# A second searched sequence for the tasks of a fused attention and state-space kernel on one core

## Chip, core, metric

The kernel runs on one core of a Trainium2 chip. The core has engines that work at the same time, each through its own list of instructions in a fixed order: TensorE (PE, matrix products; PEld is its weight load), VectorE (DVE), ScalarE (ACT), GpSimd (POOL) and SyncE (SP). The last two mostly issue transfers here. The metric is the time of one execution on the device in microseconds (us), lower is better. Three runs of the kernel before took 327.48, 326.56 and 324.36 us; the median is 326.56.

## What is computed

Two branches read the same `x` of 2,048 positions and 640 channels, and a gate mixes them. Branch A is attention over eight keys at distances 0, 2, ..., 14; branch B is a long convolution whose filter comes from 192 complex states per channel.

```python
g = sigmoid((x * gate_w).sum(-1, keepdims=True))

# A: 32 heads of 20; query s sees the keys s - 2*w, w = 0..7
q, k, v = split_heads(x @ wqkv)
idx = arange(2048)[:, None] - 2 * arange(8)[None, :]
logits = where(idx >= 0, einsum("hsd,hswd->hsw", q, k[idx]) * 20 ** -0.5, -1e9)
a = merge_heads(einsum("hsw,hswd->hsd", softmax(logits), v[idx])) @ wo

# B: K[d, l] = Re sum_n C[d,n] dB[d,n] exp(dt A[d,n] l), then y = x * K + x Dskip
dt = exp(log_dt)[:, None]
K = einsum("dn,dnl,dn->dl", C, exp((dt * A)[:, :, None] * arange(2048)), dt * B).real
b = irfft(rfft(pad(x)) * rfft(pad(K)))[:, :2048] + x * Dskip

out = g * a + (1 - g) * b
```

## The kernel before

The program is cut into tasks. Each builder adds tasks to a plan by `Plan.add`: a name, the engine or engines that may make it, the function that writes its instructions, the tasks it must follow, and the buffers it takes and frees. There are two plans, "main" with 1,258 tasks and "tail" with 304. Nothing at build time decides the sequence: `ORDER` (L54) holds, for each plan, one string of differences between task numbers. `Plan.order` walks it, and a letter behind a number names the engine (A is ACT, D is DVE, S is SP, G is POOL) where it isn't the task's first one:

```python
for x in ORDER[self.name].split():
    at += int(x.rstrip("ADSG"))
    t = self.tasks[at]
    t.eng = x[-1] if x[-1] in "ADSG" else next(iter(t.dur))
```

`Plan.emit` (L152) writes the instructions in that sequence and chains those of each engine, so the string fixes every engine's list. Ahead of an ACT task whose function is not in the table set that is loaded (exponential and logarithm in one, sine and arctangent in the other), it writes a table load (L160).

What the tasks of the main plan do, in the rough order of the data:

- *Projections.* x and the weights come into `bufA` by SP, x in four chunks of 512 positions. PE multiplies them into the PSUM tile `tb` (L284, five matmuls of 128x512 a tile), and ACT or DVE copies the tile to `qr`, `kr` or `prj` (q, k, v; `evict`, L476 on ACT and L478 on DVE). A small copy `kr<-kr` carries the last 14 keys of one block of 256 positions to the next.
- *Attention* of a block: `prod` = q times shifted k on DVE (L343), summed over a head by PE into `lg` (L349), row maximum (`mx`, `hi`, `lo`, L365 to L369), exponential into `at` on ACT (L377), row sums and 1/sum on PE and DVE (L381, L385), a way through DRAM by SP that spreads the weights over partitions (`asb`, L391 and L396), `pv` = weights times v on DVE (L417; v is loaded as `vc` by POOL, L337), summed by PE (L424), multiplied by `wo` (L448), and scaled by the gate into `ga` (L457 on ACT, L459 on DVE), which SP stores (L469).
- *State-space parameters.* DVE and ACT work out the size and angle of each state's factor from A, B, C and dt in tiles of 128x960 (builders L591 to L599, called from L639 to L691). The results, split into digits, are the pieces `pc` (L630 and others), which SP stores to `Sprm` in DRAM (L623). Ten chunks of 64 channels load them back as `L` (L734).
- *Filter.* Per chunk PE makes arguments from `L` into PSUM (`ar`, two buffers, L769), ACT takes sines of them into `big` or `bufA` (L784) and exponentials into `big` (L786), DVE multiplies these to `pt` and `qq` (L806, L808), and PE sums over the states in runs of 16 or 32 small matmuls of 32x21 into `kps` (L824), which is evicted to `E`. When five chunks are done, their half of the filter goes by way of DRAM (`Kx`) into `kc` (L907).
- *First transform step* of the filter and of x on PE into `bp` (L1276, L1295), evicted to `big` and `bufA`.

The tail plan holds the rest of the transforms: forward (`fp`, L1043, evicted to `sp_k` and `sp_u`), product of spectra on DVE (L1071, L1074), inverse (L1104, L1134), and the mix with the gate, `ga` and `Dskip` (L1140 to L1148), from which `ot` goes to the output (L1161).

PSUM tiles are few: two `ar`, two `tb` (shared by projections, gathers and output products), one `lg`, one for `kps`. So who frees a tile, and when, sets which engine waits.

## Time and profile before

| | us |
|---|---|
| three runs | 327.48, 326.56, 324.36 |
| median | 326.56 |
| span of the profiled execution | 323.2 |
| projections on PE (L284, 275 matmuls of that shape) | 73.4 |
| sines on ACT into `big` (L784, 72) | 56.1 |
| exponentials on ACT (L786, 60) | 50.4 |
| `prod` on DVE (L343, 40) | 47.8 |
| `pv` on DVE (L417, 40) | 47.6 |
| arguments on PE (L769, 600) | 47.1 |
| `pt` and `qq` on DVE (L806 48, L808 24) | 32.1 + 21.2 |
| `kps` matmuls on PE (L824, 2,560) | 28.1 |
| table loads on ACT (L160, 14) | 18.0 |

The span reaches from the first to the last thing that the profiler recorded on the core. A row of a view names engine, line, operation, output and inputs, and how often it stands there; then busy time and mean duration, or start and length, and in brackets the idle time ahead of it with what ended it ("issue" where nothing that the profile shows did). Line numbers are those of the kernel before; in the changed kernel all lines behind the table are two higher.

### The profile page before, as it was taken

The numbers are of one execution on the slowest core, as the hardware profiler recorded it, in microseconds if no ns is written. First come the engines' busy times: TensorE is split into PE (matmuls) and PEld (weight loads), VectorE is DVE, ScalarE is ACT, GpSimd is POOL, SyncE is SP. The second block draws the span as 40 slices with busy tenths as digits, with TensorE's granted clock in tenths as the row PEclk, the third lists the DMA queues.
The fourth block names the chain that finished last, engine by engine and source line by source line (L and its number), as shares of the span: only waits on it lengthen the run. The fifth ranks groups of instructions, "written<-read, shape, count | busy, mean of one in ns | idle before, by whom it ended". The sixth has DMA issues, their size and how long they took to land.

```text
span 323.2 us, 11733 instructions
## 1 busy us (share of the span) xinstructions
PE 278.4 (86%) x5109; PEld 170.3 (53%) x5134; DVE 294.0 (91%) x408; ACT 281.5 (87%) x425; POOL 62.8 (19%) x94
## 2 busy tenths in 40 slices
PE   0599997999979999999998979889999999997750
PEld 0145543444545645546554545457678776657740
DVE  4888999899998999999999989898998999999891
ACT  1479678999989999999999999899988599996991
POOL 8500026501100000111134523320200000000063
PEclk9999999999999999999999997999999999997995
DMA  8997356662414102467774996533860593962057
GB/s 213 338 227 224 122 173 138 130 128 83 92 30 109 37 6 74 81 161 254 179 190 97 161 179 141 108 96 77 254 258 33 151 312 95 204 123 44 2 135 194
DMA packets 48697, 45.65 MB, mean 141 GB/s; under 512 B 28590, under 2 KB 42482, under 8 KB 48646
## 3 DMA queue, kind: packets, MB, share of 16 engines
q1 hardware_dynamic: 42524, 27.82, 33.7%
q0 software_dynamic: 5216, 16.39, 20.8%
q8 instruction: 40, 0.66, 0.9%
q10 hardware_dynamic: 906, 0.69, 0.7%
q14 instruction: 11, 0.09, 0.1%
HBM read 28.25 MB, written 14.01 MB: 131 GB/s over the span
## 4 chain that ended last, share of the span: by engine, by line
PE 48%; ACT 39%; issue 5%; DVE 3%; SPq 2%; DMA 2%; POOL 0%; POOLq 0%; ACTq 0%; DVEq 0%
PE tb L284 14%; ACT big L784 8%; PE fp L1043 7%; PE ar L769 7%; ACT big L786 6%; PE kps L824 5%; ACT bufA L476 4%; PE tb L424 4%; PE tb L448 4%; ACT L160 3%; PE bp L1276 3%; ACT tt L1140 2%; ACT bufA L784 2%; ACT sp_k L476 2%; DMA bufA<-in_A_wqkv_dram 2%
## 5 line engine op out<-in xcount | busy, mean ns | idle before, releaser
L284 PE MATMUL tb<-bufA 128*128 128x512 bf16 x275 | 73.4, 394 | 6.5 <-DMA bufA<-in_A_wqkv_dram 2.9
L784 ACT ACTIVATE big<-ar 128x740 bf16<-128x740 int16 (+1 forms) x72 | 56.1, 849 | 2.4 <-PE ar L769 1.9
L786 ACT ACTIVATE big<-ar 128x848 bf16<-128x848 f32 x60 | 50.4, 919 | 3.2 <-PE ar L769 3.0
L769 PE MATMUL ar<-Rarg,L 64*128 64x212 bf16 (+4 forms) x600 | 47.1, 253 | 6.3 <-ACT big L784 2.5
L284 PEld LDWEIGHTS <-bufA 128*128 128x128 bf16 x300 | 32.3, 121 | 35.2 <-issue 12.0
L417 DVE TENSOR_TENSOR pv<-vc,asb 128x2048 bf16<-128x2048 bf16 x40 | 47.6, 1217 | 1.1 <-DMA vc<-vS 0.9
L343 DVE TENSOR_TENSOR prod<-qr,kr 128x2048 bf16<-128x2048 bf16 x40 | 47.8, 1218 | 0.5 <-PE lg L349 0.5
L769 PEld LDWEIGHTS <-L 64*128 64x128 bf16 x600 | 22.3, 95 | 35.0 <-issue 32.1
L806 DVE TENSOR_TENSOR pt<-big 128x1024 bf16<-128x1024 bf16 x48 | 32.1, 701 | 1.5 <-PE kps L824 0.8
L824 PE MATMUL kps<-qq,pt 128*32 128x21 bf16 (+1 forms) x2560 | 28.1, 175 | 3.3 <-issue 3.1
L824 PEld LDWEIGHTS <-pt 128*32 128x32 bf16 (+1 forms) x2560 | 23.4, 91 | 12.2 <-issue 10.1
L448 PE MATMUL tb<-wo_sb,oTm 128*128 128x320 bf16 x160 | 27.1, 300 | 0.1
L337 POOL DMA_DIRECT2D vc<-vS x16 | 11.5, 727 | 70.6 <-DVE pv L417 65.4
L476 ACT ACTIVATE sp_u<-fp 128x640 bf16<-128x640 f32 x29 | 22.4, 883 | 2.1 <-PE fp L1043 2.1
L476 ACT ACTIVATE sp_k<-fp 128x640 bf16<-128x640 f32 x30 | 22.7, 878 | 1.0 <-PE fp L1043 0.8
L424 PE MATMUL tb<-pv,ind 128*64 128x512 bf16 (+1 forms) x192 | 22.7, 359 | 0.3 <-ACT qr L476 0.2
L808 DVE TENSOR_TENSOR qq<-big 128x1344 bf16<-128x1344 bf16 x24 | 21.2, 884 | 0.0
L1043 PEld LDWEIGHTS <-PHI 128*128 128x128 bf16 x160 | 15.6, 97 | 8.1 <-issue 1.5
L1161 POOL DMA_DIRECT2D out_dram<-ot x14 | 7.8, 562 | 54.9 <-DVE ot L1143 54.9
L448 PEld LDWEIGHTS <-oTm 128*128 128x128 bf16 x160 | 14.5, 98 | 7.3 <-issue 2.7
L160 ACT ACT_TABLE_LOAD x14 | 18.0, 1283 | 0.3
L476 ACT ACTIVATE qr<-tb 128x512 bf16<-128x512 f32 (+1 forms) x22 | 10.8, 514 | 6.7 <-PE tb L284 6.7
(153 smaller groups left out, 512.0 us busy)
## 6 DMA issues: line engine op xcount, KB each, us to landing
vc<-vS POOLq DMA_DIRECT2D x16, 327.5 KB, 5.8
vS<-prj POOLq DMA_DIRECT2D x4, 640.0 KB, 5.7
gaS<-ga SPq DMA_DIRECT2D x8, 320.0 KB
Usb<-in_A_x_dram POOLq DMA_DIRECT2D x8, 320.0 KB, 5.0
gaF<-gaS SPq DMA_DIRECT2D x8, 320.0 KB
bufA<-in_A_wqkv_dram SPq DMA_DIRECT2D x3, 800.0 KB
Sprm<-pc SPq DMA_DIRECT2D x10, 240.0 KB
L<-Sprm SPq DMA_DIRECT2D x38, 60.0 KB
```

The source lines that it names most:

```text
L284: nc.tensor.matmul(ppf, self.wq[:, which, kt, e::5], self.xT[:, c0 // 1024, kt, c0 % 1024:c0 % 1024 + SC], start=(kt == 0), stop=(kt == NK ...
L343: nc.vector.tensor_tensor(b[e][:], self.qr[:, sc % NRB, e, :].unsqueeze(1).to_broadcast([128, W, C]), win(self.kr[:, sc % NRB, e, :], 0, W ...
L417: nc.vector.tensor_tensor(o, vw, b["asb"][:].unsqueeze(2).to_broadcast(sh), ALU.mult)
L424: nc.tensor.matmul(b["op", e][64 * a:64 * a + 64, 0:n, :], ind[:, 32:96], b["pv", e][:, w, a, 0:n, :], start=(w == 0), stop=(w == 3), skip ...
L448: nc.tensor.matmul(apf[:, :320], b["oT"][:, e, i * 128:(i + 1) * 128], wo_sb[:, e, hf * 320:(hf + 1) * 320], start=(e == 0), stop=(e == 4))
L476: nc.scalar.activation(o, i, ACT.Identity)
L769: nc.tensor.matmul(ar[:, g2, a0:a0 + ncol], L[rows, gv, sb, l0:l0 + 128], R[rows, c0:c0 + ncol], start=True, stop=True, tile_position=(64 ...
L784: nc.scalar.activation(d_[:, :, s0 * QW:s1 * QW], ar[:].bitcast(I16)[:, :, 0:2 * (s1 - s0) * QW:2], ACT.Sin, scale=SCL)
L786: nc.scalar.activation(dst[:, gp::2].rearrange("p g s n -> p g (s n)"), ar[:, :, 0:2 * EW], ACT.Exp)
L806: nc.vector.tensor_tensor(pt[:, :, k, :], gg[:, :, ::-1] if k else gg, e1, ALU.mult)
L824: nc.tensor.matmul(kps[32 * g:32 * g + 32, h ^ (g // 2), NM * ql:NM * ql + NM], pt[rows, k, v, :], qq[rows, k, v, :], start=(g not in star ...
L1043: nc.tensor.matmul(fp[:, fl % 2, 0:320].rearrange("p (c x) -> p c x", x=32), phis[fb][:, fl, kind, :], B[:, :, 2 * f1 + ri].rearrange("p c ...
```

## The change

Only the two strings of `ORDER` are replaced. The tasks, their instructions and what they must follow are the same; what changes is their sequence in both plans, and the engine of 65 evictions and small copies out of 1,562 tasks. Of the main string and the tail string the first line each:

```diff
 ORDER = {"main": (
-    "52 -52 3 -2 3 7 -6 -3 51 -47 6 -5 1 7 -6 45 10 1 2 -1 2 1 -14 1 -43 75 -31 -47 79 -13 -62 76 -65 52 -49 3 -15 62 -55 "
+    "61 1 -47 -15 7 -6 2 -1 4 6 -8 7 -6 59 -1 -55 5 -4 1 1142 -1138 51 -40 41 -38 24 -29 30 -37 6 -5 37 4 1 1 -13 23 -44 45 "
...
 ), "tail": (
-    "0 7 -6 1 1 1D 1 1D 5 -3 4 1 2 1 -7 5D 6 6 8 1D -25 7 124 -114 11 -20 1 2 19 -1 -9 -8 19 1 -10 -9 1 7 2 -5 1 20 1 -14 "
+    "3 2 -1D 7 -5D 7 -1D -5 2 -1D 6 -4 10 1 -6 2 -1 2 4 1 3 1 1 10 -8 -1 2D -7 10 5 -3 -1 -3 5 -4 7 1 -41 1 1 23 18 1 1 1 "
```

The numbers themselves tell nothing; the lists that come of them do, at three places.

**The state-space parameters, DVE and ACT.** DVE's list before, from the first sum of products behind the second chunk's `prod` on. `ay`, `xl`, `at` and the `t` and `x` tiles are steps of size and angle, `wi` and `wr` products of B and C, `lnd` a logarithm from ACT, `pc` the pieces that are stored.

```order
L593 TENSOR_TENSOR ay<-ay,ax 128x960
L630 TENSOR_TENSOR pc<-xa,pc 128x960
L630 TENSOR_TENSOR pc<-x_148,pc 128x960
L593 TENSOR_TENSOR t_142<-wi,t_142 128x960
L343 TENSOR_TENSOR prod<-qr,kr 128x2048
L670 SCALAR_TENSOR_TENSOR xl<-xl,lnd 128x960
L630 TENSOR_TENSOR pc<-s_152,x_148 128x960
L599 SCALAR_TENSOR_TENSOR t_142<-wr,t_142 128x960
L599 SCALAR_TENSOR_TENSOR at<-at,t_142 128x960
```

The same place of DVE's list now:

```order
L672 SCALAR_TENSOR_TENSOR xl<-xl,lnd 128x960
L595 TENSOR_TENSOR ay<-ay,ax 128x960
L595 TENSOR_TENSOR xa<-are,dtb 128x960
L632 TENSOR_TENSOR pc<-x_148,pc 128x960
L632 TENSOR_TENSOR pc<-s_152,x_148 128x960
L345 TENSOR_TENSOR prod<-qr,kr 128x2048
L595 TENSOR_TENSOR t_142<-wi,t_142 128x960
L632 TENSOR_TENSOR pc<-xa,pc 128x960
L632 TENSOR_TENSOR pc<-xl,pc 128x960
```

The step on `xl` stands ahead of `ay` now instead of five rows behind it, and pieces that need no late result from ACT are made before `t_142<-wi,t_142`, which is DVE's 24th row in both.

ACT's list before, between the gate's exponential and the first sine. `om` is the row 1 - g, `big<-ar` the sines.

```order
L476 ACTIVATE qr<-tb 128x256 x4
L476 ACTIVATE kr<-tb 128x256 x2
L377 ACTIVATE at<-lg 128x512
L231 ACTIVATE om_569<-ar 16x128
L160 ACT_TABLE_LOAD
L784 ACTIVATE big<-ar 128x2x444
```

And now:

```order
L478 ACTIVATE kr<-kr 128x5x14
L478 ACTIVATE qr<-tb 128x256 x2
L478 ACTIVATE kr<-tb 128x256 x2
L233 ACTIVATE om_559<-ar 16x128
L379 ACTIVATE at<-lg 128x512
L162 ACT_TABLE_LOAD
L786 ACTIVATE big<-ar 128x2x444
```

The exponential is the last step ahead of the table load now, and a copy of the 14 keys is ACT's. On PE, ten projection matmuls stood between the row sums of that first softmax and the first arguments; now the first arguments stand ahead of the row sums, and eight of these matmuls behind them.

**An eviction on DVE.** DVE's list before, ahead of the first row maximum; `ge` to `ob` are the gate's own steps, and `lg<-lg,oTm` sets the mask.

```order
L478 COPY kr<-kr 128x5x14
L343 TENSOR_TENSOR prod<-qr,kr 128x2048 x2
L219 TENSOR_SCALAR ge<-ge 128x16
L220 RECIPROCAL g_sb<-ge 128x16
L222 TENSOR_SCALAR omg<-g_sb 128x16
L224 CAST ob<-omg 128x16
L363 TENSOR_TENSOR lg<-lg,oTm 32x8x14
L365 TENSOR_REDUCE mx<-lg 128x64
```

And now:

```order
L221 TENSOR_SCALAR ge<-ge 128x16
L222 RECIPROCAL g_sb<-ge 128x16
L224 TENSOR_SCALAR omg<-g_sb 128x16
L226 CAST ob<-omg 128x16
L345 TENSOR_TENSOR prod<-qr,kr 128x2048
L480 CAST prj<-tb 128x512
L365 TENSOR_TENSOR lg<-lg,oTm 32x8x14
L367 TENSOR_REDUCE mx<-lg 128x64
```

The copy of the keys is gone from DVE's list, and an eviction of v into `prj` stands between the last product and the maximum. Over the whole program DVE takes on six `prj`, two `E`, one `bufA` of 512 and one eviction of the tail, and gives up two evictions of 1,024, one `qr`, two `oTm` and two copies of keys.

**The first half's filter on SP, and the runs of kps on PE.** SP's list before, around the filter's way through DRAM:

```order
L396 DMA asb<-aS 64x1x1024 x2
L734 DMA L_161<-Sprm 40x4x192 x4
L900 DMA Kx<-X 128x4x640
L901 DMA Kx<-X 64x4x640
L907 DMA kc<-Kx 128x2560
```

And now:

```order
L902 DMA Kx<-X 128x4x640
L903 DMA Kx<-X 64x4x640
L736 DMA L_157<-Sprm 40x4x192 x4
L471 DMA gaS<-ga 128x2x640
L736 DMA L_161<-Sprm 40x4x192 x4
L909 DMA kc<-Kx 128x2560
```

The load of `kc` follows its stores directly before, and stands behind two chunks' loads of L and a store of `ga` now. On PE the 2,560 small matmuls of `kps` stood in 44 runs before, with nothing of another kind inside a run: eight of 96, two of 128 and one of 144. They stand in 68 runs now, five of 96, one of 112 and one of 128; the one of 112 is in the seventh chunk, behind eight argument matmuls with two projection matmuls among them.

88 rows, old and new, of the table ORDER are left out of this document.

## Prediction

> **What bounds the kernel now.** The order of reading was: the page's busy times, the same busy times by stage, the waits of the engine that is busiest, and then the rows at the places where it waits. First the page of the kernel before: span, busy time of each engine, and the transfers that bring PE its instructions (packets, MB, share).
>
> ```profile
> span 323.2 us, 11733 instructions
> PE 278.4 (86%) x5109; PEld 170.3 (53%) x5134; DVE 294.0 (91%) x408; ACT 281.5 (87%) x425; POOL 62.8 (19%) x94
> ...
> q8 instruction: 40, 0.66, 0.9%
> ```
>
> Three engines are nearly full at once, and DVE is the fullest. Only 29.2 us of its span (323.2 - 294.0) are idle. By stage (columns: length, then busy us of PE, PEld, DVE, ACT and POOL with instruction counts, granted clock, DMA share, GB/s):
>
> ```profile
> 0.00:40.00 40.00, 27.72 (x185) 13.97 (x188) 31.57 (x35) 24.21 (x40) 11.77 (x17) 1.00 0.81 227
> 40.00:240.00 200.00, 184.37 (x3991) 106.19 (x4013) 190.57 (x273) 190.56 (x278) 42.55 (x61) 0.99 0.53 130
> 240.00:260.00 20.00, 19.32 (x151) 14.40 (x150) 17.80 (x22) 14.33 (x23) 0.75 (x2) 1.00 0.34 108
> 260.00:290.00 30.00, 29.51 (x209) 20.01 (x207) 29.76 (x41) 29.88 (x52) 0.00 (x0) 1.00 0.72 173
> 290.00:317.00 27.00, 17.51 (x581) 15.72 (x579) 24.32 (x42) 22.55 (x38) 6.25 (x12) 0.89 0.37 78
> 317.00:323.20 6.20, 0.00 (x0) 0.00 (x0) 0.00 (x0) 0.00 (x0) 1.52 (x3) 0.50 0.62 172
> ```
>
> DVE is idle for 8.4 us in the first 40, 9.4 in the next 200, 2.2 around the change of plan, 0.2 in the transforms, 2.7 behind them, and 6.2 at the end, where only stores run. So the account is made on DVE: span = its work + its idle time. An order can lower only the idle part, and can raise the work by giving DVE evictions.
>
> **The change, part by part.** No instruction's shape changes. Three things do: what stands ahead of what, which of ACT and DVE makes an eviction, and the order on the queues of SP and POOL.
>
> *The start.* These rows are DVE's and ACT's steps of the state-space parameters, then the first loads of L, then the first arguments (start, length, engine, line, out<-in, idle before):
>
> ```profile
> 22.17 1.16 DVE L593 TENSOR_TENSOR ay<-ay,ax 128x960 f32<-128x960 f32 x1 [0.47 <-ACT ay L662]
> 24.09 1.16 DVE L630 TENSOR_TENSOR pc<-xa,pc 128x960 bf16<-128x960 f32 x1 [0.77 <-ACT pc L476]
> 27.68 1.16 DVE L593 TENSOR_TENSOR t<-wi,t 128x960 f32<-128x960 f32 x1 [1.36 <-ACT t L665]
> 39.12 1.16 DVE L630 TENSOR_TENSOR pc<-t,t 128x960 bf16<-128x960 f32 x1
> 42.41 2.33 SPq L734 DMA_DIRECT2D L<-Sprm  x6
> 47.03 0.60 ACT L377 ACTIVATE at<-lg 128x512 bf16<-128x512 f32 x1
> 47.79 1.28 ACT L160 ACT_TABLE_LOAD   x1
> 47.91 2.12 PE L284 MATMUL tb<-bufA 128*128 128x512 bf16 x9
> 50.17 0.52 PE L769 MATMUL ar<-Rarg,L 64*128 64x296 bf16 x8
> 50.58 0.91 ACT L784 ACTIVATE big<-ar 128x888 bf16<-128x888 int16 x1 [1.50 <-PE ar L769]
> ```
>
> DVE waits 0.47 + 0.77 + 1.36 = 2.60 us for ACT here. In the new order `t<-wi,t` is DVE's 24th row as before, with the same work ahead, but ACT reaches the logarithm that it needs behind six evictions instead of nine, and DVE's steps on xl, which need ACT's first results alone, stand ahead of `ay`. I take 0.4 us of the 2.60 as left, so the last parameter piece ends at 40.3 - 2.2 = 38.1 instead of 40.3 (39.12 + 1.16), and the loads of L, 2.1 us behind it, go out 2.2 us earlier. On PE, most of the nine projection matmuls that took 2.12 us ahead of the first arguments stand behind them now. Then what ends last ahead of the first sine is the table load: the first softmax exponential (47.03) comes 1.5 us earlier, because DVE is 2.2 us ahead less one eviction of 0.68, and the 1.50 us that ACT waited for PE behind its table are gone. The first sine starts near 47.6, 3.0 us earlier. On DVE's account the term is **-2.2**; bounds are 0 (other waits of the same size) and -2.6.
>
> *Evictions that change the engine.* 65 tasks change, and most cancel. By the built orders DVE gains six prj, two E, one bufA (of 512) and one sp, and loses two of 1,024 elements, one qr, two oTm (512 and 256) and two halo copies. The prices on DVE:
>
> ```profile
> L478 DVE CAST big<-bp 128x1024 bf16<-128x1024 f32 x5 | 6.0, 1218 | 0.1
> L478 DVE CAST kr<-tb 128x512 bf16<-128x512 f32 x4 | 2.8, 688 | 0.3 <-PE tb L284 0.3
> L478 DVE CAST sp_u<-fp 128x640 bf16<-128x640 f32 x3 | 2.5, 822 | 0.7 <-PE fp L1043 0.7
> L478 DVE CAST E<-kps 128x336 bf16<-128x336 f32 x3 | 1.5, 506 | 1.1 <-PE kps L824 1.0
> L478 DVE CAST kr<-tb 128x256 bf16<-128x256 f32 x4 | 1.4, 416 | 0.0
> L478 DVE COPY kr<-kr 128x70 bf16<-128x70 bf16 x6 | 1.0, 174 | 0.1
> ```
>
> 6 x 0.69 + 2 x 0.51 + 0.69 + 0.82 = 6.7 on, and 2 x 1.22 + 2 x 0.69 + 0.42 + 2 x 0.17 = 4.6 off: **+2.1** of work on the fullest engine. It is not hidden, since DVE has no cover. ACT is relieved by about 2 us, which makes it the engine with slack.
>
> *DVE's waits behind the start.* From 40 us to the end of its work, the largest waits and the larger ones on ACT (engine, waiting line, releaser: us, times, longest):
>
> ```profile
> DVE ga L459 <- PE tb L448: 2.0, 4, 1.0
> DVE ot L1148 <- PE yp L1134: 1.2, 1, 1.2
> DVE rs L385 <- PE lg L381: 1.0, 2, 0.7
> DVE E L478 <- PE kps L824: 1.0, 1, 1.0
> DVE pv L417 <- DMA vc<-vS: 0.9, 1, 0.9
> DVE pt L806 <- PE kps L824: 0.8, 2, 0.4
> ...
> DVE ot L1143 <- ACT tt L1140: 0.6, 2, 0.4
> ...
> DVE pt L806 <- ACT bufA L784: 0.4, 1, 0.4
> ...
> DVE pt L806 <- ACT big L784: 0.4, 1, 0.4
> ```
>
> With ACT's sines 3 us ahead and its load 2 us lower, the waits of pt for ACT (0.4 + 0.4, and two of 0.3 that are not shown) should go: -1.4. The single waits of 1.0 in E (at 100.9) and in ga (at 209.1) each follow a pause of PE inside a run of the small kps matmuls, where nothing that the profile shows ends the pause:
>
> ```profile
> 91.47 0.36 PE L824 MATMUL kps<-qq,pt 64*32 64x21 bf16 x30
> 93.11 0.39 PE L824 MATMUL kps<-qq,pt 64*32 64x21 bf16 x34 [1.27 <-issue]
> ...
> 202.44 0.60 PE L824 MATMUL kps<-qq,pt 64*32 64x21 bf16 x59
> 204.15 0.42 PE L824 MATMUL kps<-qq,pt 64*32 64x21 bf16 x37 [1.10 <-issue]
> ```
>
> PE's 10,270 rows in 40 instruction transfers are about 257 rows each, and 64 matmuls with their loads are half a transfer in 0.36 to 0.65 us; so I read the pauses as PE running out of instructions. At both places the new order sets argument, logit or projection matmuls between the runs: -2.0. Together **-3.4**. Bounds: -9 (some three fifths of the 14.5 us that DVE is idle from 40 to 317 by the stages) and +2.6, two new pauses of 1.3 that reach DVE, since the run of chunk 6 now has 112 kps matmuls with four arguments alone among them.
>
> [...]
>
> *Clock and queues.* The clock falls once in the middle:
>
> ```profile
> 191.70:195.10 3.40, 1.99 (x102) 1.63 (x105) 3.40 (x4) 3.39 (x6) 1.49 (x2) 1.00 0.88 218
> 195.10:198.50 3.40, 3.40 (x50) 1.28 (x40) 3.04 (x6) 2.89 (x5) 1.21 (x2) 0.50 0.34 59
> ```
>
> After a stretch with PE busy for 1.99 of 3.40 us, the next is granted 0.50, and DVE loses 0.36 us in it, ACT 0.51. I cost it at nothing either way: one such stretch fewer or more is under 0.4 us on DVE. [...] On SP, the load of the first half's filter (kc) now stands behind L8 and L9. It is hidden by the work ahead of its first reader, and if that cover is gone, PE waits with all arguments behind it. In the tail plan only transforms change places; PE and DVE are both full there (29.51 and 29.76 of 30.00), so nothing is won, and one eviction of 0.82 is in the sum already.
>
> *Sum.* 323.2 - 2.2 + 2.1 - 3.4 = 319.7 for the profiled span. The median of the runs, 326.56, lies 3.4 above that span, and I leave this as it is: **323.0**.
>
> **The rivals.**
> 1. *DVE's waits only move.* DVE waits for PE more than for ACT in the rows above, PE is busy for 184.4 of 200 us, and its work is the same; then only start and work count: 326.56 - 2.2 + 2.1 = 326.5. For it: the largest waits are all on PE. Against it: ACT's head start.
> 2. *Slower: PE runs out of instructions more often.* Place: the runs of kps between arguments, above all chunk 6. Price: 1.27 us a pause (the longest row), and while PE stands ACT has two argument buffers left. From three such pauses that reach DVE the gain is gone; with four it is 326.5 + 4 x 1.27 = 331.6. For it: the run of 112. Against it: of 3.1 us of such pauses before, two of 1.0 show on DVE.
> [...]
>
> **How the numbers follow.** Forecast 0.50, rival 1 0.26, rival 2 0.14, rival 3 0.10. A measurement of this kernel can tell about 1% from no change, which is under 323.3 or over 329.8. The forecast's own range is 317 to 325, of which a little lies within 1%: faster 0.45 of its 0.50, same 0.05. Rival 1 gives 0.02 faster, 0.23 same, 0.01 slower; rival 3 0.02 faster and 0.08 same; rival 2 0.02 same and 0.12 slower. Sums: faster 0.49, same 0.38, slower 0.13. The range goes from 326.56 - 2.6 + 2.1 - 9 = 317.1 to 326.5 + 2.6 = 329.1.
>
> **What would show it.** The start is right if DVE's wait for t L665 is under 0.5 us and the first sine starts between 47 and 49 us; wrong if it starts at 50 or later. The work is right if DVE's busy time is 295.5 to 296.5. The third term is right if DVE is idle for less than 7 us between 40 and 240 (9.4 before), with no wait of 1 us behind a kps run; rival 2 is right if the waits of kps on "issue" sum to more than 5 us. The forecast is wrong if DVE stays idle for as long as before, wherever the waits lie, or if PE waits for kc.

## The result, and the profile after

| | before | changed |
|---|---|---|
| median of four runs (us) | 325.46 | 338.81 |
| lowest and highest (us) | 323.47, 327.48 | 335.81, 341.14 |
| span of the profiled execution (us) | 323.2 | 337.9 |
| mean granted clock in it | 0.976 | 0.950 |

The ratio is 1.038, with an interval of 1.028 to 1.048: slower, where 323.0 and "faster or the same" were forecast. (Ratios leave out executions over 1.5% above the fastest of their kernel, so for kernels with a wide spread they stand below the ratio of the medians.)

The page of the changed kernel, span and busy times of the engines:

```profile
span 337.9 us, 11792 instructions
...
PE 289.7 (86%) x5134; PEld 168.5 (50%) x5134; DVE 294.0 (87%) x411; ACT 281.2 (83%) x422; POOL 71.5 (21%) x94
```

DVE and ACT do the same work as before to 0.3 us. PE is busy 11.3 us longer, but not all of that is real: the trace of before lacks 25 of the 300 projection matmuls, and these rows took 73.4 us there and 81.7 here. Rows that are complete in both also took longer (arguments 49.7 us against 47.1, `kps` 30.7 against 28.1, output products 30.1 against 27.1), so part of PE's time ran at a lower clock (0.950 in the mean against 0.976). By stage, the changed kernel (columns as in the prediction):

```profile
0.00:40.00 40.00, 25.50 (x170) 12.56 (x170) 29.90 (x34) 24.10 (x37) 13.31 (x20) 0.96 0.87 226
40.00:240.00 200.00, 185.33 (x3930) 96.28 (x3930) 181.56 (x265) 177.61 (x260) 46.33 (x52) 0.96 0.49 114
240.00:268.00 28.00, 25.70 (x206) 19.49 (x204) 23.66 (x25) 24.06 (x35) 2.21 (x5) 1.00 0.40 128
268.00:337.90 69.90, 53.22 (x832) 40.18 (x831) 58.91 (x88) 55.44 (x92) 9.69 (x18) 0.90 0.60 146
```

The last stage begins with the first matmul of the tail plan (`fp`). The kernel before, with its own last two stages cut at the same event:

```profile
240.00:253.20 13.20, 12.90 (x105) 9.90 (x104) 11.85 (x15) 10.39 (x16) 0.54 (x1) 1.00 0.16 48
253.20:323.20 70.00, 53.44 (x832) 40.23 (x831) 60.03 (x89) 56.37 (x93) 7.98 (x15) 0.91 0.57 141
```

The tail takes 69.9 us against 70.0, so its new sequence costs and wins nothing. All that is lost is lost in the main plan, and on DVE it is idle time: length less busy time is 10.1 (before 8.4) in the first 40 us, 18.4 (9.4) in the next 200, 4.3 (1.3) up to the tail and 11.0 (10.0) in it. These differences sum to 14.7, the whole growth of the span. The waits of the changed kernel that are new or larger (engine, line and what it waits for: us, times, longest):

```profile
PE kps L826 <- issue: 4.8, 3, 2.9
PE bp L1278 <- DMA Usb<-in_A_x_dram: 3.5, 1, 3.5
...
PE tb L286 <- DMA bufA<-in_A_x_dram: 2.4, 1, 2.4
...
DVE ga L461 <- PE tb L450: 5.7, 3, 2.4
DVE pt L808 <- issue: 4.3, 2, 3.9
...
DVE E L480 <- PE kps L826: 3.7, 1, 3.7
```

PE has three kinds of new or longer wait, and DVE's longest waits follow from them: behind the pauses in `kps`, behind a load of x at the start, and behind `Usb`, the load of x for the transform.

**The start.** Rows of PE, ACT and DVE in time order:

```profile
22.07 1.09 ACT L666 ACTIVATE t<-ay,bc 128x960 f32<-128x960 f32 x1
23.62 7.25 PE L286 MATMUL tb<-bufA 128*128 128x512 bf16 x25 [2.37 <-DMA bufA<-in_A_x_dram]
25.66 0.60 ACT L478 ACTIVATE prj<-tb 128x512 bf16<-128x512 f32 x1 [2.49 <-PE tb L286]
26.15 0.99 ACT L667 ACTIVATE t<-t 128x960 f32<-128x960 f32 x1
27.18 1.16 DVE L595 TENSOR_TENSOR t<-wi,t 128x960 f32<-128x960 f32 x1 [2.10 <-ACT t L667]
30.27 1.16 DVE L632 TENSOR_TENSOR pc<-xa,pc 128x960 bf16<-128x960 f32 x1 [1.93 <-ACT pc L478]
40.53 1.15 DVE L632 TENSOR_TENSOR pc<-t,t 128x960 bf16<-128x960 f32 x1
50.90 5.92 ACT L786 ACTIVATE big<-ar 128x888 bf16<-128x888 int16 x8
```

The new sequence puts a projection tile of x's second chunk into PE's list ahead of tiles of the first. PE stands 2.37 us for that chunk, and ACT waits for the tile. ACT's eviction of it stands between the logarithm (L666) and the exponential `t<-t` of it (L667), and this exponential is what DVE needs. DVE waits 2.10 and 1.93 us for ACT instead of 0.47, 0.77 and 1.36; the last piece ends at 41.7 us and the first sine starts at 50.90, against 40.3 and 50.58 before.

**The pauses.** The two long ones, with the matmuls behind them and the wait of ACT:

```profile
142.71 0.31 PE L826 MATMUL kps<-qq,pt 64*32 64x21 bf16 x22
145.90 0.23 PE L826 MATMUL kps<-qq,pt 64*32 64x21 bf16 x10 [2.88 <-issue]
146.40 1.95 PE L286 MATMUL tb<-bufA 128*128 128x512 bf16 x5
148.88 1.47 ACT L786 ACTIVATE bufA<-ar 128x740 bf16<-128x740 int16 x2 [4.28 <-PE ar L771]
186.83 0.34 PE L826 MATMUL kps<-qq,pt 128*32 128x21 bf16 x26
188.46 0.23 PE L826 MATMUL kps<-qq,pt 128*32 128x21 bf16 x6 [1.28 <-issue]
191.18 1.52 PE L450 MATMUL tb<-wo_sb,oTm 128*128 128x320 bf16 x5
```

Inside a run of 32 the instructions stop for 2.88 and 1.28 us. DVE stands for 3.91 and 2.08 us behind them. The clock adds to it: at these pauses and at two waits for x PE is granted half its speed (0.50 from 23.97, 146.85, 187.81 and 232.18 us on). By the clock records of the trace this is so for 20.5 us up to 250 us, against 3.4 in the kernel before. Stretches of 3.4 us around three of these places (length, PE busy, ..., granted clock third from the end):

```profile
20.60:24.00 3.40, 1.03 (x6) 0.39 (x4) 3.40 (x5) 2.56 (x4) 0.00 (x0) 1.00 1.17 214
24.00:27.40 3.40, 3.40 (x10) 1.22 (x8) 1.30 (x2) 1.49 (x2) 0.00 (x0) 0.50 0.97 174
...
142.80:146.20 3.40, 0.52 (x36) 0.36 (x33) 0.00 (x0) 1.80 (x4) 0.00 (x0) 1.00 0.49 85
146.20:149.60 3.40, 3.40 (x35) 1.42 (x32) 3.35 (x5) 0.72 (x2) 0.00 (x0) 0.60 0.02 5
...
231.20:234.60 3.40, 1.05 (x8) 0.61 (x12) 0.40 (x1) 0.00 (x0) 0.00 (x0) 0.64 1.02 222
234.60:238.00 3.40, 3.40 (x77) 2.42 (x77) 2.60 (x13) 2.65 (x4) 0.00 (x0) 0.50 0.68 115
```

**The load of x for the transform.** POOL issues it in eight parts, each behind a small copy (`pace`, L973) that reads the part before; then PE, which needs all eight, and ACT:

```profile
178.54 8.78 POOL L973 COPY pace<-Usb 32x2 bf16<-32x2 bf16 x1
211.56 4.45 POOL L973 COPY pace<-Usb 32x2 bf16<-32x2 bf16 x1 [2.54 <-DMA Usb<-in_A_x_dram]
227.49 0.41 POOL L973 COPY pace<-Usb 32x2 bf16<-32x2 bf16 x1 [3.98 <-DMA Usb<-in_A_x_dram]
233.55 1.09 PE L1278 MATMUL bp<-F1c,Usb 128*128 128x256 bf16 x4 [3.50 <-DMA Usb<-in_A_x_dram]
234.68 1.02 ACT L478 ACTIVATE big<-bp 128x1024 bf16<-128x1024 f32 x1 [3.67 <-PE bp L1278]
```

Before, the first part was issued at 157.01 us and the longest copy took 3.35; now the first is issued at 169.55, because the last store of v, which all eight must follow, goes out at 164.82 instead of 150.60. Between the first part and its copy POOL's list also has a store to `Kx`, the load of `kc`, which waits 5.56 us for that store, and two loads of v, and two copies take 8.78 and 4.45. The copy of 8.78 ends at 187.32 us, 0.03 behind a row of DVE that ends at 187.29; from 176.3 to there DVE's rows of bf16 products stand back to back. The last part lands at 233.5, when PE has waited for 3.5 us, and half speed follows.

### The profile page after: what moved, and what is told of

Read it like the earlier page. It is cut to its first block, busy times and chain, and to the rows that moved or that the text cites. A ratio compares the mean times of both kernels' runs of the same rounds, so it can differ in the third digit from the quotient of the medians.

```text
span 337.9 us, 11792 instructions
## 1 busy us (share of the span) xinstructions
PE 289.7 (86%) x5134; PEld 168.5 (50%) x5134; DVE 294.0 (87%) x411; ACT 281.2 (83%) x422; POOL 71.5 (21%) x94
## 4 chain that ended last, share of the span: by engine, by line
PE 17%; issue 14%; DMA 11%; ACT 8%; POOL 5%; DVE 1%; POOLq 0%; ACTq 0%; DVEq 0%
PE fp L1045 10%; DMA Usb<-in_A_x_dram 10%; POOL pace L973 3%; PE bp L1278 2%; ACT bufA L478 2%; ACT tt L1142 2%; PE tb L450 2%; DMA gaS<-ga 2%; ACT big L478 1%; PE cp L1106 1%; PE tb L426 1%; ACT sp_k L478 1%; ACT ga L459 1%; PE tb L1297 1%; POOL vS L315 0%
## 5 line engine op out<-in xcount | busy, mean ns | idle before, releaser
L286 PE MATMUL tb<-bufA 128*128 128x512 bf16 x300 | 81.7, 404 | 5.8 <-DMA bufA<-in_A_wqkv_dram 3.3
L771 PE MATMUL ar<-Rarg,L 64*128 64x212 bf16 (+4 forms) x600 | 49.7, 254 | 6.2 <-ACT big L786 2.9
L286 PEld LDWEIGHTS <-bufA 128*128 128x128 bf16 x300 | 31.4, 124 | 37.7 <-issue 17.6
L771 PEld LDWEIGHTS <-L 64*128 64x128 bf16 x600 | 21.1, 94 | 37.9 <-issue 35.6
L826 PE MATMUL kps<-qq,pt 128*32 128x21 bf16 (+1 forms) x2560 | 30.7, 175 | 4.9 <-issue 4.8
L450 PE MATMUL tb<-wo_sb,oTm 128*128 128x320 bf16 x160 | 30.1, 322 | 1.3 <-ACT ga L459 1.3
L973 POOL COPY pace<-Usb 32x2 bf16<-32x2 bf16 x7 | 15.9, 2275 | 25.0 <-DMA Usb<-in_A_x_dram 25.0
L339 POOL DMA_DIRECT2D vc<-vS x16 | 11.6, 728 | 43.9 <-DVE pv L419 38.4
L478 ACT ACTIVATE big<-bp 128x1024 bf16<-128x1024 f32 x16 | 16.0, 1044 | 5.6 <-PE bp L1278 5.6
L478 ACT ACTIVATE sp_k<-fp 128x640 bf16<-128x640 f32 x27 | 19.6, 858 | 0.4 <-PE fp L1045 0.4
```

The lines of the kernel that those rows point to most:

```text
L286: nc.tensor.matmul(ppf, self.wq[:, which, kt, e::5], self.xT[:, c0 // 1024, kt, c0 % 1024:c0 % 1024 + SC], start=(kt == 0), stop=(kt == NK ...
L450: nc.tensor.matmul(apf[:, :320], b["oT"][:, e, i * 128:(i + 1) * 128], wo_sb[:, e, hf * 320:(hf + 1) * 320], start=(e == 0), stop=(e == 4))
L478: nc.scalar.activation(o, i, ACT.Identity)
L771: nc.tensor.matmul(ar[:, g2, a0:a0 + ncol], L[rows, gv, sb, l0:l0 + 128], R[rows, c0:c0 + ncol], start=True, stop=True, tile_position=(64 ...
L826: nc.tensor.matmul(kps[32 * g:32 * g + 32, h ^ (g // 2), NM * ql:NM * ql + NM], pt[rows, k, v, :], qq[rows, k, v, :], start=(g not in star ...
L973: nc.gpsimd.tensor_copy(P["pace"][32 * g0:32 * g0 + 32, :], P["Usb"][32 * g0:32 * g0 + 32, 32 * h0, 0:2])
```

## The experiments

**What the pauses are.** The weight loads and matmuls of PE can be counted in the trace: 10,268 rows in the changed kernel (in the kernel before a missing matmul is counted by its weight load). In the profiles of all kernels of this study, 27 pauses of 1.0 us or more on "issue" stand between 55 and 255 us, and every one stands at a row whose number leaves 183 to 189 when divided by 256. The trace also has the times of each of the 40 instruction transfers of 16,384 bytes. Some of the pauses (row at which PE goes on; when it entered the block of 256 rows before that; begin and end of the transfer then under way; when PE went on; us):

```
kernel    row   entered  transfer from, to   goes on
before   1981    88.48     90.47    91.69     93.11
before   7099   199.69    201.51   202.66    204.15
changed  4283   139.52    143.15   144.54    145.90
changed  6075   179.79    185.40   186.77    188.46
b_pad72  3773   120.69    121.44   122.33    123.88
```

PE goes on 1.24 to 1.81 us (median 1.42) after its block has landed, over 38 pauses of more than 0.6 us. The transfer begins about when PE enters the block before it: 0.75 us later in the median of 231 blocks in whose first microsecond the 16 DMA engines were less than 0.3 busy, 2.1 in the median of 109 blocks with 0.9 or more, and 5.65 at most (by this count a few begin up to 1.4 us before it). So PE pauses, by these counts, where it runs through 256 rows in less time than this delay, the transfer (0.9 to 1.7 us, median 1.1) and 1.4 us take together. The theory: the new sequence makes blocks that are run through quickly while data transfers fill the DMA engines. The rivals: the pauses belong to the tasks at which they stand; or the loss comes from the start, from the late load of x, or from the changed engines.

**a_pad92: blocks shifted in the changed kernel.** Small matmuls of zeros, in PE's wait for the first weights, shift every later row by 184; sequence and data stay. The first projection starts at 12.65 us instead of 12.14.

```diff
...
+        dz = pin.tile([5, 128], BF16, name="dz")
+        nc.vector.memset(dz[:], 0.0)
+        for i in range(92):
+            nc.tensor.matmul(lt[:, 0, 0:5], dz[:], dz[:, 0:5], start=(i == 0), stop=False)
-        nc.tensor.matmul(lt[:, 0, 0:5], g5[:], at_.ident[0:5, 0:5], start=True, stop=True)
+        nc.tensor.matmul(lt[:, 0, 0:5], g5[:], at_.ident[0:5, 0:5], start=False, stop=True)
...
```

> The changed kernel with 92 small matmuls more at PE's start (they multiply zeros into the sum of the gate weights' transpose, and run while PE waits for its first data), so that all later PE instructions stand 184 rows further on in the stream. The order is untouched. Theory 1, PE pauses where a block of 256 instructions ends before the next block is there: the pauses of 2.98 and 1.39 us that stand at rows 4283 and 6075 (both 187 of 256) leave these matmuls, and with them go the stretches of half clock behind them. DVE is idle for less than 4 us between 140 and 200 (8.8 us in the changed kernel by its idle gaps over 0.35 us), and the time falls from 338.8 by 4 to 8 us, to 331 to 335. A pause that is left stands at another place. Rival, the pauses belong to the kps runs or to the order: they stay at the same matmuls, and the time stays within 2 us of 338.8.

332.3 us, ratio 1.023 (1.016 to 1.030). The pauses left their tasks and stand at rows 4539, 6075 and 7353 (0.82, 3.08 and 1.56 us), for example:

```profile
179.86 0.26 PE L830 MATMUL kps<-qq,pt 128*32 128x21 bf16 x10 [3.08 <-issue]
```

The time falls as expected, but not because the pauses are shorter. They add up to 5.5 us against 4.2, and DVE is idle for 8.1 us between 140 and 200 instead of under 4. Of the 7.9 us that the profiled execution is shorter, 1.8 are idle time of DVE in the first 40 us, 3.1 from 40 to 240, where PE now waits 1.18 us for x instead of 3.50, and the rest lies behind.

**b_pad72: the same in the kernel before**, with 72 matmuls (144 rows).

> The kernel before with 72 such matmuls at PE's start, 144 rows of shift, its order untouched. By a count of how long PE took for each 256 rows in the profile of before, this shift makes blocks of 1.3 to 1.6 us (about 123, 132 and 219 us) that no transfer of instructions can keep up with. Theory 1: new pauses of 1 us or more at two places at least, and the time rises from 325.5 by 4 to 12 us, to 329 to 338. Rival, the boundaries do not matter: 325.5 within 2 us.

331.7 us, ratio 1.021 (1.014 to 1.029). Its old pauses are gone and three new ones stand at rows 3773, 4285 and 8123:

```profile
123.88 0.21 PE L828 MATMUL kps<-qq,pt 128*32 128x21 bf16 x6 [1.63 <-issue]
...
224.17 0.20 PE L828 MATMUL kps<-qq,pt 64*32 64x21 bf16 x2 [2.81 <-issue]
```

They stand near the three places that the count of blocks had given beforehand. DVE's idle time from 40 to 240 us rises from 9.4 to 15.6. A sequence that was good loses 6.4 us by nothing but where its blocks begin. In both kernels the pauses belong to the blocks, not to the tasks.

**a_wait: the load of x without the copies on POOL.** The eight parts wait for each other by semaphores.

```diff
-        else:
-            g0, h0 = (n - 1) // 2, (n - 1) % 2
-            nc.gpsimd.tensor_copy(P["pace"][32 * g0:32 * g0 + 32, :], P["Usb"][32 * g0:32 * g0 + 32, 32 * h0, 0:2])
...
+            ub[-1].waits = ub[-2:-1]
```

> The changed kernel, where each of the eight loads of x for the transform (Usb) waits for the load before it by a semaphore, and the small copies on POOL that paced them (L973) are left out. In the changed kernel these copies took 8.8 and 4.5 us twice, each until 0.04 us behind the end of a DVE operation, and the last load landed at 233.5. Theory 2, this chain is late and PE waits for it: the last load lands at 217 to 223, PE's wait of 3.50 us ahead of the first transform step of x goes and with it the half clock behind it; the time falls by 3 to 6 us, to 333 to 336. Rival, other waits take its place (the transform steps wait for ACT or DVE, or the denser loads delay the loads of v): 338.8 within 2 us.

335.4 us, ratio 1.030 (1.021 to 1.038), 3.4 less than the changed kernel by the medians; the intervals overlap. The last part is issued at 223.74 us, later than expected, but PE no longer waits for it. The long pause stays (3.45 us at row 4283), the one at 6075 is gone, and others of 1.22 and 2.05 us stand at 7097 and 8119. The profiled execution is 3.5 us shorter, and 1.6 of this is idle time of DVE in the first 40 us, where nothing was edited. So what the late load costs by itself isn't settled; this pair of profiles leaves about 2 us for it.

**a_bstart: the start of before.** The first 147 tasks in the sequence and on the engines of before, the rest as changed (`ORDER` only).

> The changed kernel, where the 147 tasks ahead of the first argument stand in the sequence of before and on the engines of before; all behind is the changed kernel's. Theory 3, the start lost about 2 us since PE waited 2.37 us for a chunk of x and ran at half clock for 3.4 us behind it: this wait goes, the two waits of DVE for ACT (2.10 and 1.93 us) fall under 2.7 in sum, and the first sine starts 1 to 3 us earlier than 50.9. If the blocks further on kept their places relative to transfers, the time would fall by 1 to 3 us, to 336 to 338. Rival, the start is hidden or the pauses further on move: the time changes by more than 3 us in either way, or not at all, while the first sine starts earlier.

336.1 us, 2.7 less by the medians, but the ratio of 1.037 (1.028 to 1.047) is that of the changed kernel, so no gain is clear of the noise. The first sine starts at 50.09 us and DVE's wait for `t<-t` is 1.25 us instead of 2.10. The long pause stays (2.56 us at row 4283), and one of 1.40 stands at 8121. If the new start loses anything, it is under 3 us.

**a_vc: transfers kept away from the block of the long pause.** Three loads that filled the DMA engines there (`asb` of block 3, `vc` of position 768, L of chunk 7) are moved behind a run of `kps` on the far side of the boundary and wait for it.

```diff
+        named = {t.name: t for t in pl.tasks}
+        for name in ('asb3', 'vc768', 'L7'):
+            named[name].waits = [named["kmm413"]]
```

> The changed kernel, where three transfers that were under way at 137 to 145 us (the load vc768 of v on POOL, the spread asb3 of attention weights and the load L7 on SP) wait by a semaphore for the kps task (row 4301) just behind the pause of 2.98 us at row 4283; their readers come 20 us later or more. Theory 1a, the instruction transfer of that block began 3.63 us after PE entered the block before because these transfers filled the DMA engines: it begins within 1.5 us now, the pause falls under 0.7 us, DVE's idle gap of 3.91 at 142.3 under 1 us, the half clock at 146 is gone, and the time falls by 3 to 6 us, to 333 to 336. Rival, the late instruction transfer has nothing to do with other transfers: the pause stays, and the time is 338.8 within 2 us.

330.8 us, ratio 1.015 (1.010 to 1.021): 8.0 less than the changed kernel by three transfers held back. The changed kernel's stretches of 1 us while the block is due (DMA share is the last number but one):

```profile
141.00:142.00 1.00, 1.00 (x14) 0.62 (x12) 1.00 (x2) 1.00 (x2) 0.00 (x0) 1.00 1.16 246
...
143.00:144.00 1.00, 0.02 (x2) 0.00 (x0) 0.00 (x0) 1.00 (x2) 0.00 (x0) 1.00 0.92 140
```

And a_vc's:

```profile
141.00:142.00 1.00, 1.00 (x12) 0.48 (x10) 1.00 (x3) 1.00 (x3) 0.00 (x0) 1.00 0.00 0
...
143.00:144.00 1.00, 1.00 (x42) 0.62 (x39) 0.44 (x1) 1.00 (x3) 0.24 (x1) 1.00 0.00 0
```

With the engines free the instruction transfer begins 0.97 us after PE enters the block instead of 3.63, and no pause of 1 us on "issue" is left from 55 to 255 us. DVE's idle time from 40 to 240 us is 10.3 us, against 18.4 in the changed kernel and 9.4 before:

```profile
40.00:240.00 200.00, 189.41 (x4004) 101.34 (x4002) 189.68 (x274) 186.32 (x272) 48.89 (x56) 0.99 0.51 123
```

The gain is more than the 4.2 us of the two pauses that are gone, and more than the 3 to 6 expected; the half-speed stretches behind them are gone too (6.8 us of half speed up to 250 us instead of 20.5). The pause at row 6075 went though nothing was held for its block: the transfer began 2.57 us after PE entered the block before it instead of 5.61, probably since what follows the first pause now meets other transfers. That part was not aimed at. PE's wait for x, 3.50 us, stays.

**b_vc: the same idea in the kernel before.** The loads `vc` of positions 512 and 1536 are held behind its two pauses.

```diff
+        for name in ('vc512',):
+            named[name].waits = [named["kmm113"]]
+        for name in ('vc1536',):
+            named[name].waits = [named["kmm811"]]
```

> The kernel before, where two loads of v (vc512, issued at 85.2, and vc1536, issued at 198.7) wait by a semaphore for the kps tasks just behind its two pauses (1.27 us at row 1981, 1.10 at row 7099). Theory 1a: both pauses fall under 0.5 us, DVE's waits of 1.02 for E and 0.97 for ga go, and the time falls by 1 to 2.5 us, to 323 to 324.5. Rival, the pauses stay or move, or DVE does not gain from them: 325.3 within 1 us.

322.8 us over 12 runs against 325.0, ratio 0.994 (0.990 to 0.997). This is 0.6% faster than the kernel before, a small gain but clear of the noise. DVE's idle time from 40 to 240 us is 6.7 us instead of 9.4. The runs of `kps` in which the pauses of 1.27 and 1.10 us stood are unbroken:

```profile
90.98 0.65 PE L825 MATMUL kps<-qq,pt 64*32 64x21 bf16 x64
...
199.69 0.93 PE L825 MATMUL kps<-qq,pt 64*32 64x21 bf16 x96
```

**a_all: three cures at once.** The start of before, the semaphores of a_wait and 96 small matmuls at PE's start.

> The changed kernel with three edits together: its first 147 tasks in the sequence and on the engines of before, the loads of x for the transform paced by semaphores in place of POOL copies, and 96 matmuls of zeros at PE's start (192 rows of shift). Alone, 92 such matmuls gave -6.5, the pacing -3.4, the start -2.7 us against 338.8. If these are separate causes and make up the loss, the sum is 326 to 328.5 and the three stretches of half clock at 24, 146 and 234 are gone. Rival, pauses turn up at other rows because every edit moves blocks against transfers: 329 to 335, with one or more pauses over 1 us, each at a row that is 185 to 189 of 256.

334.0 us, ratio 1.026 (1.021 to 1.031). The rival held: new pauses of 1.05, 2.76 and 2.07 us at rows 5051, 6075 and 7099. Each cure shifts transfers or blocks against each other, and a shift alone does not take them apart.

**a_beng: the changed sequence with the engines of before** for the 65 tasks.

> The changed kernel's sequence with every task on the engine of before (56 tasks of the main plan and 9 of the tail go back). Theory 1, idle time and not DVE's work lost the time: DVE's busy time is 1 to 2.5 us lower than 294.0, ACT's higher by about as much, and the time stays within 3 us of 338.8, with the pauses at rows 4283 and 6075 still there. Rival, the evictions on DVE hold up PE's tiles: the time falls by more than 3 us with the pauses in place.

351.9 us, ratio 1.080 (1.074 to 1.085): 13 us slower still, which nothing had expected. DVE's busy time is 293.6, so the work is not the reason. Evictions that are back on DVE stand in its list ahead of PE's matmuls for them. DVE stands 4.00 us at one, and PE then 2.10 for a `qq` that is behind it in DVE's list:

```profile
108.52 0.69 DVE L480 CAST qr<-tb 128x512 bf16<-128x512 f32 x1 [4.00 <-PE tb L286]
...
111.81 0.35 PE L826 MATMUL kps<-qq,pt 64*32 64x21 bf16 x29 [2.10 <-DVE qq L810]
```

The engine of an eviction belongs to the sequence for which it was chosen.

**a_vcw and a_vcwb: what a_vc left.** a_vcw is a_vc with the semaphores of a_wait; a_vcwb also has the start of before.

> The changed kernel with the three transfers held back behind row 4301 (330.8 us alone) and, besides, the loads of x for the transform paced by semaphores in place of POOL copies (-3.4 alone). With the held transfers PE still waited 3.77 us for the last of these loads at 221.7, and half clock followed. Theory 2: that wait falls under 1 us, the half clock at 224 goes, and the time falls by 2.5 to 4.5 us against 330.8, to 326 to 328.5. Rival, a pause for instructions or another wait takes its place: 330.8 within 1.5 us.

> As the run before, and the 147 tasks ahead of the first argument in the sequence and on the engines of before. If late instructions, the late loads of x and the start are all that the change lost against before, the time is 323.5 to 326.5, no more than 1.5 us from 325.0. Rival, something further is lost: 327 or more, with DVE idle for more than 3 us between 60 and 240 us or more than 4 us between 240 and 270.

Medians 332.0 (four runs from 326.46 to 334.52; ratio 1.013, 1.005 to 1.021, from two of them) and 331.4 (324.85 to 334.04; too wide a spread for a ratio): no gain over a_vc. The wait for x is gone from both, but a_vcw's profile has pauses of 2.34, 1.94 and 1.80 us at rows 6331, 7097 and 8119, and a_vcwb's 1.10 and 2.09 at 6075 and 8121. The lowest run of each comes close to the kernel before or is as fast. The profiles are of executions of 333.7 and 332.9 us, so what those lowest runs looked like isn't known.

**a_warm: the price of half speed at the start.** a_vc with 12 matmuls of zeros in PE's wait for x, so that PE isn't idle there, and 116 small ones at the start, which with the 12 make up 256 rows and leave the blocks where they were.

```diff
...
+                        if first and k0 == 0:
+                            for i in range(12):
+                                nc.tensor.matmul(ppf, self.wz[:], self.wq[:, 0, 0, 0:512], start=(i == 0), stop=False)
...
```

> The changed kernel with the three transfers held back (330.8 us alone), where PE makes 12 matmuls of 512 columns with zero weights while it waits for the second chunk of x at 20.5 us, and 116 small ones at its start, so that all later rows stand exactly 256 further on and meet the same block boundaries. Nothing else is changed, so this prices the half clock behind that wait. Theory, the half clock costs: the projections behind the wait take 0.22 us each from the first on and not 0.43, DVE's two idle gaps there (3.07 and 1.74 us) fall by 1.5 to 3 us in sum, and the time by as much, to 327.5 to 329.5. Rival, PE makes it up later: 330.8 within 1 us.

329.5 us, ratio 1.017 (1.014 to 1.021). The median is 1.25 us under that of a_vc, but the ratio, each time to runs of the kernel before made beside it, is not lower than a_vc's 1.015. So no gain is clear of the noise. The 25 projection matmuls behind the wait in a_vc:

```profile
23.93 7.25 PE L286 MATMUL tb<-bufA 128*128 128x512 bf16 x25 [2.98 <-DMA bufA<-in_A_x_dram]
```

And in a_warm:

```profile
23.84 5.62 PE L292 MATMUL tb<-bufA 128*128 128x512 bf16 x25
```

They take 5.62 us instead of 7.25, DVE's two waits for ACT fall from 3.07 + 1.74 to 0.55 + 1.00, and the first sine starts at 49.42 instead of 51.21. But half speed at this place does not come with the sequence alone. a_wait has the start of the changed kernel without these matmuls; PE waits longer for the chunk there, is idle for most of a stretch of 3.4 us, and goes on at full speed:

```profile
23.33 5.63 PE L286 MATMUL tb<-bufA 128*128 128x512 bf16 x25 [3.01 <-DMA bufA<-in_A_x_dram]
...
20.60:24.00 3.40, 0.67 (x4) 0.40 (x5) 3.40 (x5) 1.64 (x3) 0.00 (x0) 1.00 1.16 216
24.00:27.40 3.40, 3.40 (x17) 1.85 (x16) 2.19 (x2) 2.60 (x5) 0.00 (x0) 1.00 0.99 183
```

DVE's idle time in the first 40 us is 8.5 us there and the first sine starts at 48.93; a_vcw, with the same start again, has 8.3 and 48.83. The clock records show one difference. The half-speed stretches of one execution begin at whole multiples of 3.413 us from one another (in the changed kernel at 23.97, 146.85 and 187.81), and this grid lies differently in each execution (counted from the start of the span, 0.07 us behind a whole multiple in the changed kernel, 0.52 before). In the changed kernel one step of it, from 20.55 to 23.97, holds the whole wait, and PE is busy for 31% of the step. In a_wait the wait is shared by two steps, with 62 and 49%. So it looks like chance whether the start is slowed. No run tests this, and no sharp limit comes out: a step with 43% was not followed by half speed in a_beng, and one with 58% was in the kernel before.

**a_hold and a_hold2: all short blocks kept free.** a_hold is a_vcwb with more loads (`vc`, L, `asb` and a part of x) held behind four short blocks; a_hold2 also holds another part of x and one more `vc`, and frees one part.

```diff
+        for name in ('vc1024', 'L9', 'rows1', 'asb4'):
+            named[name].waits = named[name].waits + [named["kmm701"]]
+        for name in ('vc1280',):
+            named[name].waits = named[name].waits + [named["kmm812"]]
...
```

> The changed kernel with the start of before, the loads of x for the transform paced by semaphores, and transfers held back at all four short blocks: asb3, vc768 and L7 until behind row 4301; vc1024, L9, asb4 and the second load of x until behind row 6085; vc1280 until behind row 7127; vc1792 until behind row 8149; and the last two loads of x ahead of vc1536 on POOL. Engines and all else of the order are the changed kernel's. In the runs without the last three holds (326.5 to 334.5 and 324.9 to 334.0) the pauses at rows 6075, 7099 and 8121 came and went. Theory 1a: with no transfers in flight at these blocks the pauses fall under 0.7 us each, and the time is steady at 322 to 326, that of before. Rival, the sequence itself has further losses, or the held transfers are late for their readers: 328 or more, with waits of DVE for vc, asb or kps.

> The kernel of the run before with the holds set by where its two remaining pauses stood (2.08 us at row 6843, with the third load of x in flight, and 3.77 us at row 8119, with vc1536 and the last load of x in flight): the second load of x goes ahead of vc1024 and is not held, the fourth load of x is held behind row 6843, and vc1536 behind row 8149. Theory 1a, pauses behind transfers are what is left of the loss: no pause over 1 us is left at a block's end between 60 and 240 us, DVE's idle gaps from 190 to 240 (9.1 us in that run) fall under 4 us, and the time to 322 to 327. Rival, the sequence loses elsewhere as well, or the loads of x now come too late for the transform steps: 328 or more without such pauses, or with PE waiting for x.

331.4 us (six runs from 327.19 to 335.99; ratio 1.011, 1.006 to 1.016, from three of them) and 332.7 (1.023, 1.017 to 1.028). a_hold lost the pauses at 6075 and 7099 and got others of 1.99 us at 6843 and 3.67 at 8119, where a `vc` and the last part of x were under way. a_hold2 has no pause over 1 us at the end of a block, but the held loads come late: PE waits 2.77 us for x, and DVE 2.0 for `vc`.

```profile
225.03 0.65 PE L1275 MATMUL bp<-F1c,Usb 128*128 128x256 bf16 x4 [2.77 <-DMA Usb<-in_A_x_dram]
...
DVE pv L419 <- DMA vc<-vS: 2.0, 1, 2.0
```

So in this sequence a load that is held comes too late and one that isn't held pushes an instruction block aside: x is loaded from 165 us on in eight parts of some 5 us each, in the same stretch as the short blocks. Not settled is whether the sequence without either would be level with the kernel before. The lowest run of a_vcwb (324.85) suggests it, and no profile shows it.

## Why the prediction was wrong, point by point

*The start (-2.2).* Not won. The count is right: the logarithm stands behind six evictions instead of nine. The step that failed is to let DVE's wait follow from this count. DVE reads the exponential of the logarithm, a seventh eviction stands between the two, and what that one waits for was not looked at: a tile of x's second chunk, which had not landed. In the profiled execution DVE's idle time in the first 40 us rose by 1.7 us (10.1 against 8.4), and by the prediction's own test (first sine at 50 us or later) the step is wrong. Some of this is the half speed that this execution met. In a_wait and a_vcw, which start alike without it, DVE still waits 1.11 and 0.93 us for the exponential and 1.00 for the piece behind it, instead of 0.4 in all, and is idle for as long as before, though the first sine starts 1.7 us earlier. So the term measured from about 0 to +2.0 (a_vc), and not -2.2.

*Evictions (+2.1).* The DVE rows of the evictions sum to 41.6 us against 39.6, nearly as worked out. They didn't show in the page's busy time, which stayed at 294.0 instead of 295.5 to 296.5, since the page counts overlapping rows once (all rows of DVE sum to 322.0 against 320.4). Two us of work decided little where DVE was idle for 43.9. That the engines could be priced as work alone was wrong: a_beng puts them back and loses 13 us by waits.

*DVE's waits (-3.4).* The reading that PE runs out of instructions was right, and a_vc, b_vc and the two shifted kernels show it. (Two slips in its working change nothing: PE has 10,268 rows, and the 0.36 us belongs to 30 matmuls, not to 64.) What failed is "at both places the new order sets argument, logit or projection matmuls between the runs: -2.0". A pause is not a property of the tasks beside a run. It depends on how long PE takes over 256 rows, and on how full the DMA engines are when the next block is due. The block boundaries could have been worked out from the order and the delay from the instruction transfers of before; how full the DMA engines would be, only in part. The -1.4 for waits on ACT didn't come either: `pt` waits once, for 1.2 us, where it waited 0.4, 0.4 and 0.3 (the fourth wait that the prediction adds was one of `E`). The idle time from 40 to 240 us became 18.4, not under 7.

*Rival 2* had the mechanism and the sign, with the wrong place and price. By its own sign it just missed: the waits of `kps` on "issue" sum to 4.8 us, not to more than 5. The run of 112 in chunk 6 has no pause. The price was read from the longest pause of before, 1.27 us; the longest now is 2.88, and DVE stands 3.91 behind it. Its forecast of 331.6 left out both the half-speed stretches and the load of x. The bound of two new pauses of 1.3 us was too low for the same reason.

*Which blocks come late.* Most come in time: of the 31 blocks that PE enters between 55 and 255 us, two ended in a pause of 1 us or more in the kernel before and two in the changed one. These four were late beside busy DMA engines (share 0.75 to 1.06 from PE's entering the block ahead to the begin of the transfer), and in b_pad72 one came late that PE ran towards through a block of 1.6 us beside quiet ones (entered at 120.69 us, on at 123.88; DMA share 0.04 from 119.0 to 122.4).

*Clock (nothing).* Not borne out. It was priced by one stretch more or fewer; it became 20.5 us of half speed up to 250 us instead of 3.4. In the changed kernel it falls 0.35 and 0.95 us after PE has come out of a wait (at 23.97 and 146.85), and while PE still stands (at 187.81 and 232.18); what stands behind PE there is late already. Its price apart from those waits is not shown: a_warm takes one such stretch away and wins nothing that is clear of the noise.

*Queues.* The load of `kc` is hidden as said: no wait of PE for it. The load of x on POOL was not looked at, though its order behind the last store of v could be read from the lists; it cost PE 3.5 us and DVE 3.7 in waits. What it is worth alone is not settled by a_wait.

*The tail plan* was costed at nothing, and is (69.9 against 70.0).

Put together: the one part that a single edit shows clear of the noise is a_vc's 8.0 us, pauses with their half speed, of a loss of 13. What makes up the other 5 us or so stays open. a_vc still has the wait for x, behind which DVE stands for 3.77 us, and 10.4 us of idle time in the first 40, but a_vcw and a_vcwb, without these, are no faster, since pauses turn up elsewhere. The single cures don't add up.

## What to carry to other kernels

Where PE runs many small matmuls, work out how long it takes over each 256 rows of its list, and keep large transfers away from the moment at which it enters a block that is short: under 3.3 us of work, by an estimate from the medians above (0.75 + 1.1 + 1.42), plus the delay that full DMA engines add (3.63 instead of 0.97 us in the case of a_vc). A change of order is judged by what each early row waits for (here a chunk of x and a chain of paced loads), not by how many rows stand ahead of it. A kernel whose time hangs on such boundaries moves by 2% when rows are only shifted (331.7 against 325.3 us in b_pad72, 332.3 against 338.8 in a_pad92), so a comparison of two sequences says little until the pauses have been looked for in both. Nor does one profile price a stage: the same start took 8.3 to 10.4 us of DVE's idle time in four profiles.

## What the runs showed of the hardware

- The transfer of an instruction block that PE needs came later beside data transfers: it began 0.75 us (median) after PE entered the block before in quiet stretches and up to 5.65 us after with full DMA engines, and PE went on 1.42 us (median) after it had ended. Holding three transfers back took one delay from 3.63 (changed kernel) to 0.97 us (a_vc).
- A copy of 32x2 elements on POOL took 8.78 us in the changed kernel while DVE's bf16 products ran back to back, and ended within 0.04 us of the end of a DVE row, as did the one of 4.45. No DVE row in these two stretches lasts over 1.22 us, so each copy spanned several of them. Behind the row at whose end the copy ended, DVE stood idle, for 2.08 and 0.32 us. What ties the two engines is not shown.
- Half speed (0.50) followed stretches of 3.41 us in which PE had been busy for 1.05, 0.95, 1.78 and 1.29 us (changed kernel, before 23.97, 146.85, 187.81 and 232.18), and not only stretches without work. It did not follow one in a_wait with 0.67 of 3.40 us. The half-speed stretches begin at whole multiples of 3.413 us from one another, at another offset in each profile, and in a_wait two such steps share the wait, with PE busy for 62 and 49% of them. That this is what spared a_wait is the author's reading, which no run tests.
